# Leaving out 36 of the 70 clock-keeping products of an attention-and-expert kernel

## The chip, the cores and the metric

The kernel runs on one core of one Trainium2 chip. The metric is device time in microseconds of one execution. A core has a matmul engine (PE; its weight loads stand apart as PEld), VectorE (DVE), ScalarE (ACT), GpSimd (POOL) and SyncE (SP), each with its own instruction queue that is worked off in order, and DMA queues that move data. The engines wait for each other through semaphores. [...]

## The reference: what is computed

There are four batches of eight heads, each with 768 positions of 64 channels. For each head, six projected sign bits put every query and every key in one of 64 buckets, and a query attends only to the keys of its own bucket. The eight heads of a batch are laid side by side into rows of 512. Of each batch, the 128 rows with the highest gate score go through a two-layer expert and are added back.

In short:

```python
q_bits = (np.einsum('bhsd,dk->bhsk', q, proj) > 0).astype(np.int64)
k_bits = (np.einsum('bhsd,dk->bhsk', k, proj) > 0).astype(np.int64)
mask = q_bucket[:, :, :, None] == k_bucket[:, :, None, :]
scores = np.where(mask, scale * np.matmul(q, k.transpose(0, 1, 3, 2)), -1e9)
scores = scores - np.max(scores, axis=-1, keepdims=True)
attn = np.exp(scores); attn = attn / (attn.sum(-1, keepdims=True) + 1e-09)
x = np.matmul(attn, v)          # heads side by side: (4, 768, 512)
top_idx = np.argpartition(-(x[b] @ w_gate), 128)[:128]
out[b, top_idx] = xe + sigmoid(score) * (np.maximum(xe @ w1, 0) @ w2)
```

## The kernel before, in words

The 32 heads go through the same stages. In the **max pass** of a head (max_unit L649, max_relu L657, max_red L666) each of six row chunks takes two products of 128x384 into PSUM banks; ScalarE makes the tile me of one, and DVE joins it with the other and leaves the row maxima in one column of the tile M. The tiles me have two buffers, so the third me of a series waits until DVE has read the first. The maxima are turned into a row (row_first L462 for the first head, max_turn L676 for the others), which ScalarE copies into row 96 of the head's operand A (L466 for the first head). With that row in place come the **score products** (st_unit L697, L701), the exponentials on ScalarE (L715, L717), the low halves R on DVE and POOL (L732, L735) and the products with the values (av L760). The max pass of the next head is interleaved with the score and value products of this one. Four PSUM banks ("bank") serve the max pass, three ("st") the score products, one ("av") the values.

The first head has nothing to be interleaved with. While its inputs are still being split, PE computes its sign bits (hash_first L397) and those of the next heads (hash_half L476), and the max products come in between, as DVE and ScalarE let banks come free.

The **clock-keeping products** stand between these. `keep_warm` takes an st bank and calls `heat`, which multiplies a tile of ones by itself, 128x128 each time; nothing reads the result. There are six groups, of 34, 8, 8, 8, 6 and 6 products (in the trace: tile wq, L307). The group of 34 follows the first head's sign products. The three groups of 8 lie inside the first head's max pass. The two groups of 6 are PE's last instructions, behind the last product of the last batch's expert (down L993, tile yp).

The order of everything is written out by hand: a list of events is built once (`ev`), and the table `ORDER` names them by number in the order in which they are recorded. Each engine executes its share in that order. Leaving five events out of the list lowers the numbers behind them by five.

Of the kernel before, what the change touches and what calls it, by code (L numbers as in the profile page):

```python
# [44 lines left out]
WARM = (34, 8, 8, 8, 6, 6)  # L45
# [6 lines left out]
    0, 25, 8, 17, 31, 32, 33, 159, 9, 23, 15, 36, 10, 24, 26, 34, 91, 35, 309, 18, 158, 161, 308,  # L52
    28, 114, 163, 90, 1, 42, 92, 2, 44, 93, 164, 3, 160, 310, 95, 43, 94, 45, 96, 46, 48, 47, 99,
    -1, 97, 115, 102, 98, 49, 104, 100, 38, 107, 101, 103, 311, 106, 105, 12, 4, 165, 37, 166,
    110, 108, 20, 112, 22, 27, 111, 19, 29, 109, 39, 172, 113, 21, 16, 176, 173, 174, 178, 30,
    177, 314, 180, 120, 122, 192, 7, 179, 182, 124, 121, 123, 126, 116, 233, 128, 125, 175, 194,
    466, 130, 127, 117, 14, 181, 193, 162, 184, 129, 465, 118, 131, 5, 138, 11, 183, 264, 167,
    234, 136, 186, 140, 132, 119, 168, 133, 185, 188, 195, 187, 190, -1, 134, 189, 191, 13, 256,
    390, 260, 615, 261, 262, 143, 139, 258, 169, 170, 248, 252, 263, 144, 257, 146, 135, 145, 265,
    171, 147, 254, 259, 245, 137, 266, 148, 468, 244, 253, 141, 255, 150, 149, 196, 142, 246, -1,  # L60
    152, 198, 313, 315, -1, 197, 250, 316, 616, 241, 199, 200, 421, 247, 240, 202, 242, 151, 153,
    154, -1, 249, 201, 214, 471, 208, 267, 210, 155, 235, 209, 203, 236, 268, 243, 251, 211, 50,
    237, 334, 212, 238, 239, 326, 336, 204, 51, 213, 269, 217, 335, 327, 328, 337, 156, 338, 329,
    52, 330, 340, 339, 205, 323, 272, 206, -1, 270, 157, 218, 341, 207, 332, 53, 331, 220, 391,
    322, 271, 342, 765, 276, 273, 317, 219, 344, 221, 618, 278, 274, 215, 277, 312, 333, 915, 222,
    467, 216, 473, 343, 324, 397, 223, 280, 345, 325, 224, 275, 413, 470, 398, -1, -1, 225, 319,
    399, 318, 282, 320, 414, 321, 226, 227, 288, 279, 415, 229, 228, 401, 281, -1, 416, 230, 400,
    417, 290, 283, 403, 409, 232, -1, 346, 284, 231, 402, 472, 916, 404, 286, 419, 285, 347, 418,
    411, 289, 293, 410, 287, 420, 294, 405, 348, 295, 412, 422, 296, 407, 479, 392, 291, 499, 620,
    350, 480, 297, 299, 481, 500, 482, -1, 292, 298, 300, 301, 352, 349, 6, 351, 406, 501, 423,  # L70
    408, 358, 354, 364, 302, 303, 304, 393, 483, 394, 359, 502, 305, 353, 360, 541, 495, 355, 395,
    484, 485, 306, 486, 469, 424, 307, 356, 357, 487, 425, 361, 396, 540, 362, 491, 474, 493, 363,
    489, 368, 1223, 367, 365, 369, 371, 373, 488, 366, 427, 617, 496, 433, 490, 426, 370, 428,
    497, 492, -1, 429, 559, 548, 435, 498, 551, 430, 434, 494, 375, 552, 621, 553, 372, 431, 476,
    561, -1, 437, 619, 374, 475, 766, 436, 623, 432, 622, 438, 554, 377, 477, 376, 447, -1, 378,
    571, 379, 555, 547, 54, -1, 549, 445, 380, 441, 478, 550, 55, 382, 564, 381, 439, 556, 443,
    557, 1072, 450, 560, 446, 440, 558, 562, 503, 442, 768, 542, 451, 444, 563, 567, 453, 691,
    384, 565, 452, -1, 569, 56, 633, 504, 448, 383, 543, 507, 566, 57, 509, 638, 568, 505, 572,
    455, 457, 570, 637, 635, 510, 459, 385, 454, 449, 506, 515, 639, 770, 508, 544, -1, 545, 387,
    511, 456, 629, 634, 458, 461, 546, 521, 640, 460, 512, 631, 513, 630, 517, 641, 462, 649, 636,  # L80
    516, 514, 690, 632, 518, 643, 389, 645, 519, 646, 522, 579, 463, 577, 1073, 464, 520, 578,
    642, 525, 581, 523, 573, 651, 526, 524, 585, 528, 580, 650, 721, 624, 644, 647, 717, 582, 530,
    -1, 589, 648, 527, 697, 705, 652, 767, 532, 699, 719, 698, 595, 529, 590, 718, 700, 583, 626,
    625, 531, -1, 591, 771, 574, 627, 707, 584, 586, 706, 772, 713, 575, -1, 533, 769, 708, 592,
    534, 715, 536, 628, 720, 535, 701, 537, 587, -1, 593, 588, 597, 539, 714, 596, 576, 538, 594,
    653, 655, 702, 716, 654, 709, 600, 602, 773, 711, 601, 657, 722, 840, 656, 703, 603, 598, 599,
    604, 791, -1, 659, 658, 723, 671, 710, 605, 607, 783, 918, 712, 704, 660, 609, 606, 611, 785,
    608, 610, 692, 1222, 917, 661, 694, -1, 695, 784, 779, 612, 662, 663, 792, 781, 786, 793, 664,
    920, 665, 667, 780, 794, 693, 666, 613, 782, 696, 795, 668, 841, 669, 724, 388, 614, 739, 788,
    787, 797, 672, 921, 725, 727, 923, 670, 674, 386, 673, 675, 728, 677, 789, 676, 679, 678, 922,  # L90
    774, 1075, 796, 729, 726, -1, 798, 800, 855, 730, 680, 799, 790, 740, 681, 801, 731, 732, 857,
    733, 735, -1, 682, 683, 734, 1078, 847, 802, 856, 848, 849, 684, 736, 745, 919, 776, 777, 858,
    737, 775, 778, 741, 686, 685, 859, 738, 851, -1, 743, 850, 867, 687, 852, 871, 853, 868, 869,
    998, 864, 689, 803, 854, 747, 860, 870, 688, 804, 746, 863, 865, 750, -2, 751, 861, 866, 752,
    862, 945, 754, 753, 742, 805, 744, 806, 947, 809, 929, 842, 748, 811, 749, 843, 844, 807, 810,
    756, 931, 812, -1, 758, -2, 755, 757, 845, 808, 813, 846, 930, 58, 759, 761, 814, 59, 760,
    932, 762, 946, 872, 1074, 817, 933, 815, 60, 819, 1522, 935, 816, 950, 934, 818, 763, 924,
    885, 948, -1, 61, 873, 820, 949, 764, 821, 877, 937, 951, 822, 879, 825, -2, 823, 1028, 878,
    997, 952, 826, 827, 829, -2, 824, 828, 1225, 883, 941, 936, 880, 939, 942, 943, 884, 944, -2,
    830, 874, 881, 1080, 938, -1, 886, 925, 891, 940, 831, 1004, 1012, 926, 1077, 1076, 887, 833,  # L100
    927, 832, 882, 888, 1008, 835, 834, 928, 1079, 1014, 895, 889, 875, 890, 1006, 897, 836, 1013,
    955, 893, 1005, 896, 837, 1015, 892, -2, 959, 1017, 839, 1007, 876, 838, 1016, 1018, 900,
    1010, 901, 1009, 1024, 1086, 1019, 903, 1148, 1011, 960, 1025, 1026, 999, 894, 1088, 953, 902,
    -1, -2, 1020, -2, 1228, 954, 898, -2, 1029, 905, -2, 1373, 904, 1027, 907, 957, 961, 1147,
    1224, 956, 958, 1021, -2, -2, 971, 965, 909, 962, 906, 1022, 966, 963, 1000, 1090, -1, 899,
    1087, 964, 908, 910, 911, 1023, 1094, 1092, 1089, 1001, 1095, 967, 912, -2, -2, 1096, 1097,
    1098, 1002, -2, 913, 969, 1106, 1099, 914, 1091, 1100, 968, 975, 1003, -1, 1030, 1375, 1178,
    976, 1040, 970, 972, -1, 973, 1093, 978, 1034, 977, 1154, 979, 1101, 980, 1035, 1048, 1108,
    1107, 1229, 1102, 1041, 974, 1109, 1036, 1104, 1103, 1156, 1081, 982, 1105, 1155, 1158, 1037,
    1038, -1, 981, 1157, 1372, 1031, 1083, -2, 1227, 1082, 1162, 1039, 1164, 1046, 1042, 1167, -1,  # L110
    1160, 1230, 1084, 984, 1159, 1052, 986, 983, 985, 1032, 1047, 1161, 1166, 1049, 1043, 1168,
    987, 1053, 1169, 1044, 1050, 1045, 1054, 1175, 989, 1085, 1033, -2, 1110, 1124, 1523, 1297,
    -2, 988, 1174, 1236, 1163, 1176, 1057, 1177, 990, 1170, 1051, 1058, 1059, 1240, 1055, 1060,
    1112, 1378, 1061, 1111, 1298, 1056, 1172, 1171, 1122, 1165, 1179, 1113, 1123, 1063, 1062,
    1173, 1064, 1125, 1226, 1149, 1065, 1114, 1066, 1067, 1068, 1069, 1151, 1238, 1241, 1126,
    1374, 1115, 1242, 1243, 1116, 1152, 1150, 1237, 1128, 1117, 62, 1239, 64, 1118, 1308, -1,
    1071, 1070, 1248, 63, 1244, 1119, 1120, 1121, 65, 1132, 1133, 1135, 1153, 1246, -6, 1134,
    1245, 1127, 1129, 1186, 1231, 1310, 1130, 1180, 1247, 1196, 1136, 1380, 1131, 1184, 1197,
    1680, 1185, 1249, 1190, 1181, 1188, 1250, 1251, 1309, -6, -1, 1138, 1232, 1379, 1182, 1679,
    1137, 1139, 1187, 1257, 1256, 1140, 1258, 1142, 1311, 1141, -6, 1143, 1183, 1252, 1259, 1144,  # L120
    1192, 1316, 1253, 1191, 1198, 1189, 1324, 1254, 1317, 1193, 1318, 1194, -6, 1255, 1199, 1200,
    -1, 1319, 991, 1146, 1304, -6, 1326, 1305, 1299, -6, 1195, 1306, 1145, 1204, 1202, -1, 1233,
# [1186 lines left out]
```

## Time and profile before

| | |
|---|---|
| median of 3 runs | 411.87 us (411.31 to 412.36) |
| the profiled execution | 410.81 us, of which its span 408.6 us |
| PE busy | 389.4 us (95% of the span), 5738 products |
| DVE busy | 347.4 us (85%) |
| ACT busy | 332.2 us (81%) |
| POOL busy | 184.0 us (45%) |
| granted PE clock, mean | 1.00 |

The durations that follow are of the one profiled execution. The span runs from its first to its last instruction, and what the execution's own time has beyond it, 2.2 us, lies around it. A product that is followed by others shows a duration longer than the distance to the next start, because products overlap: for a run of them, the distance between starts is what each of them costs.

### The profile page before, as it was taken

How to read it: one execution, taken by the hardware profiler on the slowest of the kernel's cores; microseconds unless marked ns; L12 is line 12 of the kernel's file. 1: busy time of each engine (PE TensorE's matmuls, PEld its weight loads, DVE VectorE, ACT ScalarE, POOL GpSimd, SP SyncE). 2: the span in 40 equal slices, each digit the busy share in tenths (PEclk: the TensorE clock that was granted, in tenths of full speed). 3: DMA queues.
4: the chain of work that ended last, by engine and by line, in shares of the span. 5: the costliest groups of instructions: out<-in, count | busy, mean ns of one | idle time of the engine just before them, and what ended most of it. 6: DMA issues, size and time to landing. Idle time of an engine off the chain costs nothing.

```text
span 408.6 us, 14314 instructions
## 1 busy us (share of the span) xinstructions
PE 389.4 (95%) x5738; PEld 275.8 (68%) x5746; DVE 347.4 (85%) x928; ACT 332.2 (81%) x818; POOL 184.0 (45%) x105
## 2 busy tenths in 40 slices
PE   5799999999989999999999998999999999999995
PEld 3355776666756667687667765676677677778782
DVE  5998998998888998878889899999989988759942
ACT  5699999899989989897689987999899887757410
POOL 7737467466534466461523525335436260511010
PEclk9999999999999999999999999999999999999999
DMA  8475758655365666545455533834555354100030
GB/s 247 143 231 146 202 156 225 187 165 158 73 209 142 166 163 185 174 106 157 107 168 140 140 99 101 224 88 123 169 141 144 68 132 118 40 3 2 34 124 27
DMA packets 25586, 55.44 MB, mean 136 GB/s; under 512 B 3818, under 2 KB 10550, under 8 KB 25520
## 3 DMA queue, kind: packets, MB, share of 16 engines
q1 hardware_dynamic: 15104, 35.97, 33.9%
q10 hardware_dynamic: 9680, 16.45, 12.8%
q0 software_dynamic: 736, 2.11, 1.6%
q8 instruction: 45, 0.74, 0.7%
q14 instruction: 21, 0.17, 0.1%
HBM read 26.19 MB, written 7.35 MB: 82 GB/s over the span
## 4 chain that ended last, share of the span: by engine, by line
PE 75%; DVE 9%; issue 7%; ACT 5%; DMA 3%; POOLq 0%; SPq 0%; DVEq 0%; ACTq 0%
PE av L760 23%; PE st L697 14%; PE st L701 13%; PE bank L649 13%; PE bank L969 4%; PE bank L476 3%; PE bank L993 2%; DVE mj L666 2%; ACT me L657 1%; DVE R L732 1%; PE av L744 1%; ACT x L784 1%; DVE sel L896 1%; ACT P L715 1%; DVE cm L838 1%
## 5 line engine op out<-in xcount | busy, mean ns | idle before, releaser
L735 POOL TENSOR_TENSOR R<-P 128x1536 f16<-128x1536 f32 x46 | 134.1, 2918 | 158.9 <-DVE R L732 36.4
L760 PEld LDWEIGHTS <-P 128*128 128x128 bf16 x2304 | 127.2, 97 | 30.6 <-issue 4.3
L760 PE MATMUL av<-V,P 128*128 128x65 f16 (+2 forms) x2304 | 135.1, 194 | 0.1
L760 PE MATMUL av<-V,R 128*128 128x65 f16 (+1 forms) x1152 | 128.0, 193 | 1.0 <-DVE R L732 0.9
L666 DVE CUSTOM_DVE_ANT_0 mj<-bank,me 128x384 bf16<-128x384 f32 x192 | 102.4, 551 | 26.2 <-ACT me L657 12.0
L715 ACT ACTIVATE P<-st 128x512 f32<-128x512 f32 x192 | 113.2, 612 | 13.4 <-PE st L701 9.6
L697 PE MATMUL st<-A 97*128 97x512 f16 (+1 forms) x384 | 119.8, 326 | 1.7 <-DMA A<-mr 1.1
L701 PE MATMUL st<-B 128*128 128x512 f16 (+1 forms) x384 | 120.0, 326 | 0.0
L657 ACT ACTIVATE me<-bank 128x384 f32<-128x384 f32 x192 | 94.7, 505 | 24.0 <-PE bank L649 14.9
L649 PE MATMUL bank<-A 96*128 96x384 f16 x384 | 108.7, 326 | 2.2 <-DVE sg L493 0.9
L760 PEld LDWEIGHTS <-R 128*128 128x128 f16 x1152 | 107.3, 99 | 1.6 <-DVE R L732 1.5
L732 DVE TENSOR_TENSOR R<-P 128x768 f16<-128x768 f32 x100 | 100.1, 1016 | 3.2 <-ACT P L717 2.3
L717 ACT ACTIVATE P<-st 128x512 f32<-128x512 f32 x96 | 58.4, 615 | 2.1 <-PE st L701 1.7
L649 PEld LDWEIGHTS <-A 96*128 96x128 f16 x384 | 34.8, 98 | 24.6 <-issue 6.9
L697 PEld LDWEIGHTS <-A 97*128 97x128 f16 x384 | 37.4, 97 | 17.9 <-issue 3.8
L701 PEld LDWEIGHTS <-B 128*128 128x128 f16 x384 | 37.6, 98 | 15.9 <-issue 2.1
L784 ACT ACTIVATE x<-av,rc 128x64 f32<-128x64 f32 x192 | 44.0, 324 | 2.7 <-DVE rc L772 2.0
L513 DVE SCALAR_TENSOR_TENSOR T<-X,T 128x768 f16<-128x768 f32 x32 | 31.4, 988 | 0.0
L506 ACT ACTIVATE T<-X 128x768 f16<-128x768 f32 x32 | 27.6, 867 | 0.0
L821 POOL TENSOR_TENSOR w1l<-W,w1h 128x512 bf16<-128x512 f32 x8 | 13.8, 1730 | 10.9 <-PE st L701 5.8
L969 PEld LDWEIGHTS <-w1h 128*128 128x128 f16 x256 | 15.7, 97 | 1.3
L566 DVE SCALAR_TENSOR_TENSOR V<-V,V 128x768 f16<-128x768 f32 x16 | 16.4, 1022 | 0.0
(134 smaller groups left out, 412.4 us busy)
## 6 DMA issues: line engine op xcount, KB each, us to landing
X<-in_qk_dram SPq DMA_DIRECT2D x32, 384.0 KB
B<-T SPq DMA_DIRECT2D x62, 192.0 KB
A<-T SPq DMA_DIRECT2D x31, 240.0 KB
V<-in_v_dram ACTq DMA_DIRECT2D x16, 384.0 KB
out_dram<-x ACTq DMA_DIRECT2D x7, 768.0 KB
W<-in_w_dram ACTq DMA_DIRECT2D x8, 512.0 KB
sbc<-scores SPq DMA_DIRECT2D x3, 384.0 KB
out_dram<-x SPq DMA_DIRECT2D x1, 768.0 KB
```

Of the source, the lines that this page charges most:

```text
L649: nc.tensor.matmul(pt[:, :384], a[0][0:96, t * P : (t + 1) * P], a[1][0:96, 384:768] if i else K[h % NA][0:96], start=True, stop=True,)
L657: nc.scalar.activation(me, st["mx", h, t, 0][:, :384], AF.Relu)
L666: nc.vector.tensor_tensor_reduce(out=jk, in0=st["mx", h, t, 1][:, :384], in1=st["me", h, t], op0=ALU.add, op1=ALU.max, scale=1.0 / MS, sca ...
L697: nc.tensor.matmul(pt[:, o : o + n], a[1][:, c * P : (c + 1) * P], a[0][:, q0 : q0 + n], start=True, stop=False,)
L701: nc.tensor.matmul(pt[:, o : o + n], bt[:, 0, c * P : (c + 1) * P], bt[:, 1, q0 : q0 + n], start=False, stop=True,)
L715: nc.scalar.activation(pp[:, r, 0:512], pt, AF.Exp, scale=ES)
L717: nc.scalar.activation(pp[:, :, 512:768], pt.rearrange("p (a b) -> p a b", a=2), AF.Exp, scale=ES)
L732: mine(nc.vector.tensor_tensor(t[:, r], pp[:, r], hi_view(pp, r), op=ALU.subtract))
L735: turn(nc.gpsimd.tensor_tensor(t, pp, hi_view(pp, a), op=ALU.subtract))
L760: nc.tensor.matmul(o[:, t, o0:o1], l, vv[:, c, hh, v0 + o0 : v0 + o1], start=False, stop=last and l is lo, skip_group_check=True,)
L784: nc.scalar.activation(x[:, t], o[:, t, 1 : D + 1], AF.Copy, scale=rc[:, t : t + 1])
L969: nc.tensor.matmul(hp[:, f * P : (f + 1) * P], w[:, k, o : o + P], x[:, k * P : (k + 1) * P], start=(f == 0 and k == 0 and i == order[0]), ...
```

## The change

The list of groups is cut to the first one. The 24 products inside the first head's max pass and the 12 at the end go, each with its weight load: 36 products and 36 loads on PE, and nothing on any other engine. The table ORDER loses its five entries for them, and every number from 38 up is lowered by five.

```diff
-WARM = (34, 8, 8, 8, 6, 6)
+WARM = (34,)
...
 ORDER = (
...
-    -5, -8, -5, -8, -5, -5, -5, 41, 40,
...
+    -8, -5, -8, -5, -5, -5,
 )
```

PE's queue at the third group of 8, before. bank is a PSUM bank of the max pass, A_91 and A_92 are the operands of the first and the second head, wq is the clock-keeping products' bank:

```order
 L649 LDWEIGHTS A_91
 L649 MATMUL bank_66<-A_91 128x384 [waits Activation_49]
 L307 LDWEIGHTS ones_78
 L307 MATMUL wq_279<-ones_78 128x128 [waits PE_49]
...
 L649 LDWEIGHTS A_92 [waits DMAHW5_49,DMAHW2_49,DMAHW4_49,DMASW0_49,Pool_49]
 L649 MATMUL bank_65<-A_92 128x384 [waits Activation_49]
 L649 LDWEIGHTS A_92
 L649 MATMUL bank_67<-A_92 128x384 [waits Activation_49]
```

And the same place now:

```order
 L649 LDWEIGHTS A_91
 L649 MATMUL bank_66<-A_91 128x384 [waits Activation_49]
 L649 LDWEIGHTS A_92 [waits DMAHW5_49,DMAHW2_49,DMAHW4_49,DMASW0_49,Pool_49]
 L649 MATMUL bank_65<-A_92 128x384 [waits Activation_49]
 L649 LDWEIGHTS A_92
 L649 MATMUL bank_67<-A_92 128x384 [waits Activation_49]
```

The eight pairs are gone, and the second head's first max products follow the first head's last one directly, with the same banks and the same waits. At the first two groups it is alike.

PE's queue at its end before, where hth and htl are the expert's hidden layer in two parts and yp its result:

```order
 L993 LDWEIGHTS htl_8712
 L993 MATMUL yp_8771<-w2h,htl_8712 128x512
 L307 LDWEIGHTS ones_78
 L307 MATMUL wq_8799<-ones_78 128x128 [waits PE_49]
...
 L307 LDWEIGHTS ones_78
 L307 MATMUL wq_8806<-ones_78 128x128
 L1304 UNCONDITIONAL_BRANCH
```

And now:

```order
 L993 LDWEIGHTS htl_8685
 L993 MATMUL yp_8744<-w2h,htl_8685 128x512
 L1304 UNCONDITIONAL_BRANCH
```

The twelve pairs are gone, and PE's last instruction is the expert's last product.

## Rows read from the trace of the kernel before

**Rows 1.** The page's first part, busy time, share of the span and instructions of each engine, and of its second part the slices of PE and of the granted clock (tenths, 40 slices).

```profile
PE 389.4 (95%) x5738; PEld 275.8 (68%) x5746; DVE 347.4 (85%) x928; ACT 332.2 (81%) x818; POOL 184.0 (45%) x105
...
PE   5799999999989999999999998999999999999995
...
PEclk9999999999999999999999999999999999999999
```

**Rows 2.** The timeline of PE from its first product to the second group of 8: start, duration of the run, engine, line, operation, tiles, count, and in brackets PE's idle time before it with what ended it.

```profile
4.21 1.51 PE L397 MATMUL bank<-Xa,pjt 96*32 96x384 f32 x8 [4.21 <-DMA Xa<-in_qk_dram]
5.65 3.72 PE L307 MATMUL wq<-ones 128*128 128x128 f16 x34
9.56 0.48 PE L649 MATMUL bank<-A 96*128 96x384 f16 x2 [0.20 <-DVE A L418]
...
15.42 0.32 PE L649 MATMUL bank<-A 96*128 96x384 f16 x1 [0.91 <-DVE sg L493]
...
16.18 0.61 PE L307 MATMUL wq<-ones 128*128 128x128 f16 x8
```

**Rows 3.** The chain of waits from 16 us to the first score product, in order of time: start, duration, what the chain goes through.

```profile
16.00 0.57 DVE sg L493
16.59 0.37 DVE sg L499
16.98 0.36 DVE sg L500
17.37 0.56 DVE mj L666
17.94 0.47 DVE mj L666
18.42 0.25 DVE ident L350
...
18.71 0.33 PE bank L462 x3
19.04 0.17 PE bank L649
19.20 0.45 PE wq L307 x8
19.65 0.18 PE bank L649
19.86 0.43 ACT me L657
...
20.33 0.49 ACT me L657
20.85 0.48 ACT A L466
```

**Rows 4.** The timeline of all engines from 16.6 to 21.4 us, the same columns as Rows 2 (lines of POOL, SP and the weight loads are among those left out).

```profile
16.63 0.65 PE L649 MATMUL bank<-A 96*128 96x384 f16 x3
...
17.12 0.61 PE L307 MATMUL wq<-ones 128*128 128x128 f16 x8
...
18.00 0.32 PE L649 MATMUL bank<-A 96*128 96x384 f16 x1 [0.26 <-DVE M L666]
18.04 0.97 ACT L657 ACTIVATE me<-bank 128x384 f32<-128x384 f32 x2 [0.43 <-DVE M L666]
...
19.04 0.61 PE L307 MATMUL wq<-ones 128*128 128x128 f16 x8
19.08 0.47 ACT L466 CAST A<-bank 1x384 f16<-1x384 f32 x1
19.19 0.56 DVE L666 CUSTOM_DVE_ANT_0 mj<-bank,me 128x384 bf16<-128x384 f32 x1 [0.53 <-PE bank L462]
19.49 0.65 PE L649 MATMUL bank<-A 96*128 96x384 f16 x3
...
19.67 0.55 DVE L666 CUSTOM_DVE_ANT_0 mj<-bank,me 128x384 bf16<-128x384 f32 x1
19.86 0.97 ACT L657 ACTIVATE me<-bank 128x384 f32<-128x384 f32 x2 [0.30 <-PE bank L649]
...
21.37 0.38 PE L697 MATMUL st<-A 97*128 97x512 f16 x1 [0.17 <-ACT A L466]
```

**Rows 5.** The end of the timeline.

```profile
402.46 1.03 PE L993 MATMUL yp<-w2h,htl 128*128 128x512 f16 x4
...
403.32 0.83 PE L307 MATMUL wq<-ones 128*128 128x128 f16 x12
403.52 0.75 DVE L1000 SCALAR_TENSOR_TENSOR ye<-yp,ss,xe 128x512 f32<-128x512 f32 x1 [2.63 <-PE yp L993]
404.55 0.98 POOL L1001 DMA_INDIRECT out_dram<-ye,idx  x1 [8.42 <-DVE ye L1000]
```

**Rows 6.** PE by stretches: the stretch, its length, PE's busy time with the count of products, granted clock, share and rate of the DMA engines. The stretch from 14.2 to 21.4 us stands in the table of all products here.

```profile
4.20:9.40 5.20, 5.16 (x42) 1.00 1.01 333
...
14.20:21.40 7.20, 4.96 (x46) 1.00 0.62 186
```

**Rows 7.** The same stretch of 7.2 us, the clock-keeping products (L307) alone.

```profile
14.20:21.40 7.20, 1.83 (x24) 1.00 0.62 186
```

**Rows 8.** PE by stretches at the end, the same columns.

```profile
404.20:406.00 1.80, 0.00 (x0) 1.00 0.00 0
...
408.20:408.40 0.20, 0.00 (x0) 1.00 0.00 0
408.40:408.60 0.20, 0.00 (x0) 0.74 0.00 0
```

**Rows 9.** The first 8 us of score products and value products, busy time of each engine with the count (PE, PEld, DVE, ACT, POOL), granted clock, DMA share and rate.

```profile
21.40:29.40 8.00, 7.81 (x71) 4.57 (x70) 7.60 (x21) 7.71 (x18) 3.47 (x2) 1.00 0.77 219
```

**Rows 10.** The timeline of PE at its longest wait behind the first head, the same columns as Rows 2.

```profile
251.69 0.22 PE L676 MATMUL bank<-ident,M 128*128 128x128 f16 x1 [1.43 <-DVE W L622]
...
252.33 0.27 PE L697 MATMUL st<-A 97*128 97x256 f16 x1
252.44 0.27 PE L701 MATMUL st<-B 128*128 128x256 f16 x1
```

318 rows, old and new, of the table ORDER are left out of this document.

## The prediction

> **What bounds the kernel now.** I read the page's busy times first, then the chain of waits, then the timeline of the two places where the removed products stand, and last the stretches with PE's busy time and its granted clock. The busy times show PE at 95% of the span [rows 1]: over most of the kernel what PE executes sets the time, and a product less would be time gained. The slices say where that is not so: the first slices stand at 5, 7 and 9 tenths, the last at 5, and 24 of the removed products lie in the second and third slice, 12 in the last. Both places are those in which PE waits for others.
>
> In the first place the chain shows who is waited for [rows 3]. From 16.00 to 18.67 us it is DVE alone, one instruction behind the other. Then come three transposing products, a max product, the third group of clock-keeping products (0.45 us), a max product, two me copies on ACT, and the copy that writes the row into A; at 21.37 us the first score product starts, and it had waited for that copy [rows 4]. From there PE is the bound: 7.81 of the next 8.00 us are busy [rows 9]. So a change in the first head's max pass is worth what it does to 21.37 us. At the other end DVE starts the last result at 403.52 us, when the last real product has ended (402.46 + 1.03 = 403.49), while the 12 products still execute until 404.15 us [rows 5].
>
> **The change part by part.** A run of 8 products takes 0.61 us with the last one's drain, which also stands in each run: with 0.22 us for a single product of this shape [rows 10], (0.61 - 0.22) / 7 = 0.056 us from start to start. A group therefore holds PE for 8 x 0.056 = 0.45 us, which is also what the chain shows for the third; the three hold it for 1.34 us of the 1.83 us that they show as busy [rows 7]. The 12 hold it for 0.83 - 0.22 = 0.61 us and one more distance, 0.67 us. These are the most that can be gained, 2.0 us, if all of it were waited for.
>
> First group, 16.18 to 16.63 us [rows 2, 4]. The three max products behind it start 0.45 us earlier at best. Their readers are DVE and ACT. DVE is in the unbroken row of the chain from 16.00 us [rows 3], so it comes to these banks no earlier. ACT's next me copies start at 18.04 us after a wait for DVE, for there are two me buffers [rows 4]. Cost on the path 0, gain 0.
>
> Second group, 17.12 to 17.6 us. The max product behind it starts at 18.00 us and had itself waited 0.26 us for DVE [rows 4]. Without the group it waits 0.71 us. Gain 0.
>
> Third group, 19.04 to 19.49 us. This is the one that stands in the chain [rows 3]. The second head's first max product starts at 19.49 us behind it, and ACT's me copy at 19.86 us is put down to that product, after 0.30 us of idling [rows 4]. Without the group the product could end before ACT is free of the row copy at 19.55 us (19.08 + 0.47), and the 0.30 us looks like a gain. But that me is the third of its series: it needs the buffer that DVE reads from 19.19 to 19.75 us. The two other such releases show what comes between DVE's end and ACT's start: 19.67 + 0.55 = 20.22 us to the second copy at 20.33 us, 0.11 us, and 19.75 + 0.11 is 19.86 us, the very start that the row has. So both releasers come together within hundredths, and with the product gone early DVE is the one that is late. DVE in turn starts at 19.19 us after the transposing products, which stand ahead of the group in PE's queue. Gain 0, at most the 0.30 us if the buffer is not what I take it for.
>
> The 12 at the end. DVE waits for the tile yp, not for wq, and what follows is DVE, POOL's scatter issue at 404.55 us and its transfer to 408.6 us [rows 5]. PE's queue ends 4.4 us ahead of the span's end with the group, and about 5 us without. Gain 0.
>
> The sum is 0.0 us. The profiled execution took 410.81 us (span 408.6 us and 2.2 us around it) and lies 1.06 us below the median of the runs; the change is set against the median 411.87 us, so the forecast is 411.9 us.
>
> What hides the cost of the removal is the clock. The products do no work, but they are a part of PE's activity: in the 7.2 us from 14.2 to 21.4 us PE is busy 4.96 us with them [rows 6], and 4.96 - 1.83 = 3.13 us, 43%, without [rows 7]. [...]
>
> The trace does not show so thin a stretch, so its cost is bounded from both sides. Nothing: PE stood entirely idle from 404.15 us, the rows say 1.00 until 408.4 us, and only then 0.74, a fall within the last 0.2 us [rows 8], so 4.3 us of idling went ahead of it. Without the groups the longest idle stretch is the 0.91 us that is already there, and a wait of 1.43 us in the middle left the distances of the score products behind it at 0.11 us for 256 columns [rows 10]. The other end is the fall in this stretch, priced below at 0.15 to 2.7 us. I take nothing, as the rows on idling are nearest.
>
> [...]
>
> **The rivals.** Slower: the clock falls in the first head. The place is PE between 14.2 and 21.4 us, and it decides when the level is low as the score products begin. For it speaks that the removed products were over a third of PE's busy time there (1.83 of 4.96 us); against it, 4.3 us of level kept in full idleness. Price: before 21.37 us only the three transposing products are on the path, 3 x (0.106 - 0.056) = 0.15 us. From 21.37 us PE is the bound, and if the level comes back as at the start, after 5.16 us of work, half of these are lost, 2.6 us. ACT and DVE are busy 7.71 and 7.60 of the 8 us there [rows 9], so neither makes it good. Sum 0.15 us if the level is back by then, 2.7 us if not: 412.0 to 414.6 us, mostly the latter.
>
> Faster: PE's queue was the bound after all. The chain names the third group, 0.45 us [rows 3]; a me buffer or a bank that comes free earlier than I read would give its 0.3 to 0.45 us, 411.4 to 411.6 us. If what waits on DVE were itself late because of the first two groups, up to 1.34 us, and with the end's 0.67 us up to 2.0 us, 409.9 us. Against it: the waits for DVE in [rows 4], and the DVE row without a break in [rows 3].
>
> The groups don't do what they are called: that is the forecast itself for the 24, which then keep nothing, and it is sure for the 12, behind which no product stands.
>
> **How the numbers follow.** Nothing on the path and no fall: 0.58, 411.9 us. A fall: 0.28, of which 0.03 stay below 0.3% (1.2 us, about what a measurement of this kernel can tell from no change). A gain on PE's queue: 0.14, of which 0.10 above 0.3%, since a shifted order in the first head can carry into later waits. So same is 0.58 + 0.03 + 0.04 = 0.65, slower 0.25, faster 0.10. The forecast alone has 411.3 to 412.4 us, the spread of the runs before. The range takes in the fall up to 414.5 us, and below it half of the gain, down to 410.8 us; about 0.06 and 0.08 are left out.
>
> **What would show it.** If the steps hold, the first score product starts at 21.4 us within 0.2 us, the second head's first me copy is put down to DVE instead of PE, PE's idle time in the first head grows by about 1.3 us, and the score products behind it keep their distance of 0.22 us for 512 columns. The DVE instruction of the last result starts 0.03 us behind the last yp product, and PE's level falls some 0.6 us earlier at the end. A granted clock below 1.00, or score products 0.43 us apart from 21 us on, would show the fall; a start before 21.1 us the gain. Wrong would be a time above 413.1 us or below 410.6 us.

## The result, and the profile after

| | before | after |
|---|---|---|
| median of 14 runs each, on one chip | 411.75 us (410.46 to 412.68) | 414.21 us (412.31 to 417.04) |
| ratio, 95% interval | | 1.0064 (1.0041 to 1.0087) |
| the profiled execution | 410.81 us, span 408.6 us | 413.71 us, span 411.5 us |
| mean granted clock of the profiled execution | 1.00 | 0.991 |

The change makes the kernel slower by 0.64%. The forecast was 411.9 us. The time lies inside the range (410.8 to 414.5 us) only because the range takes in a rival; it lies above 413.1 us, which the prediction itself named as a sign of being wrong. The likeliest case, no change, did not come; the rival that was given 0.28 did: PE's clock falls in the first head. Of all runs below, three (two of the kernel before, one of e5) took over 1.5% longer than the fastest of their kernel; the ratios, and the counts of runs by their clock, leave them out.

The page after, the same lines as [rows 1]; in the second and third slice the clock has lost a digit or two:

```profile
PE 390.4 (95%) x5710; PEld 273.8 (67%) x5710; DVE 347.1 (84%) x928; ACT 332.9 (81%) x818; POOL 184.3 (45%) x105
...
PE   4699999999989999999999998999999999999995
...
PEclk9879999999999999999999999999999999999999
```

PE executes 36 products fewer (the loads fall by 36; of the products of before, eight have no record), and its busy time is 1.0 us longer. The stretches after (columns as in [rows 6]: length, PE's busy time with the count, granted clock, DMA) place the low level:

```profile
17.00:18.00 1.00, 0.58 (x3) 0.99 0.09 19
18.00:19.00 1.00, 0.48 (x1) 0.50 0.47 125
...
24.00:25.00 1.00, 1.00 (x7) 0.60 0.20 53
25.00:26.00 1.00, 1.00 (x8) 1.00 0.27 61
```

The profile gives the granted clock as a share of full speed: it is 1.00 until 18.0 us, 0.50 until 24.8 us (the low level in what follows), and 1.00 again. PE's timeline over the same time, to be set against [rows 2, 4]:

```profile
4.52 1.51 PE L397 MATMUL bank<-Xa,pjt 96*32 96x384 f32 x8 [4.52 <-DMA Xa<-in_qk_dram]
5.96 2.90 PE L307 MATMUL wq<-ones 128*128 128x128 f16 x34
9.88 0.48 PE L649 MATMUL bank<-A 96*128 96x384 f16 x2 [1.01 <-DVE A L418]
...
15.74 0.32 PE L649 MATMUL bank<-A 96*128 96x384 f16 x1 [0.91 <-DVE sg L493]
16.34 0.32 PE L649 MATMUL bank<-A 96*128 96x384 f16 x1 [0.28 <-DVE M L666]
16.93 0.65 PE L649 MATMUL bank<-A 96*128 96x384 f16 x3 [0.27 <-DVE sg L493]
18.32 0.48 PE L649 MATMUL bank<-A 96*128 96x384 f16 x1 [0.73 <-DVE M L666]
19.04 0.48 PE L462 MATMUL bank<-ident,M 128*128 128x128 f16 x3 [0.24 <-DVE ident L350]
19.31 1.57 PE L649 MATMUL bank<-A 96*128 96x384 f16 x4
...
21.84 0.59 PE L697 MATMUL st<-A 97*128 97x512 f16 x1
22.23 0.63 PE L701 MATMUL st<-B 128*128 128x512 f16 x1
22.65 0.63 PE L697 MATMUL st<-A 97*128 97x512 f16 x1
```

A single max product takes 0.32 us until 17 us and 0.48 us from 18 us on. The score products that stood 0.22 us apart (21.37 and 21.59 us before) stand 0.39 to 0.43 us apart. Between the first product and the fall no idle stretch is longer than 1.01 us; that one ends at 9.88 us, 8 us ahead of the fall. In the 4 us ahead of the fall the longest is 0.91 us, and that one is there before the change too.

Where the 2.9 us between the two profiled spans lie is read by taking one instruction of each head, the product that opens its bank of value products (L744), in both timelines. The first head's, before and then after:

```profile
27.38 0.33 PE L744 MATMUL av<-W,zs 128*128 128x396 f16 x1
...
29.27 0.33 PE L744 MATMUL av<-W,zs 128*128 128x396 f16 x1
```

0.31 us are there already at the first product, which waits for the inputs (4.52 against 4.21 us); at the first head's L744 the difference is 1.89 us; at the second 2.13 us; it stays within 0.1 us of that for ten heads; 0.5 us come at 148 to 159 us and 0.4 us between 307 and 327 us, and the last head has 2.95 us. So 1.8 us of the 2.9 arise between 4.5 and 42 us, the stretch with the low level. In the profiles of e2 and e10, which also lack the three groups, it is 1.75 us each by the second head. The later steps come with the clock at 1.00. Such steps are there without any fall too: of the 1.3 us by which e1's profiled span exceeds the one before, 1.1 us come between 72 and 84 us. The last step of the changed kernel is this wait:

```profile
319.52 0.39 PE L697 MATMUL st<-A 97*128 97x512 f16 x1 [0.65 <-DMA A<-mr]
```

### The profile page after: what moved, and what is told of

The parts are those of the page before. It is cut to its first block, busy times and chain, and to the rows that moved or that the text cites. A ratio compares the mean times of both kernels' runs of the same rounds, so it can differ in the third digit from the quotient of the medians.

```text
span 411.5 us, 14249 instructions
## 1 busy us (share of the span) xinstructions
PE 390.4 (95%) x5710; PEld 273.8 (67%) x5710; DVE 347.1 (84%) x928; ACT 332.9 (81%) x818; POOL 184.3 (45%) x105
## 4 chain that ended last, share of the span: by engine, by line
PE 70%; DVE 9%; ACT 8%; issue 7%; DMA 4%; POOLq 0%; SPq 0%; DVEq 0%; ACTq 0%
PE av L760 21%; PE st L697 13%; PE st L701 12%; PE bank L649 12%; PE bank L969 4%; PE bank L476 3%; PE bank L993 3%; DMA A<-mr 2%; DVE mj L666 2%; ACT me L657 2%; ACT x L784 2%; ACT P L715 2%; DVE R L732 1%; PE av L744 1%; ACT P L717 1%
## 5 line engine op out<-in xcount | busy, mean ns | idle before, releaser
L657 ACT ACTIVATE me<-bank 128x384 f32<-128x384 f32 x192 | 94.8, 506 | 24.8 <-PE bank L649 14.0
L649 PE MATMUL bank<-A 96*128 96x384 f16 x384 | 109.9, 330 | 3.6 <-DVE sg L493 1.2
```

The source lines that it names most:

```text
L649: nc.tensor.matmul(pt[:, :384], a[0][0:96, t * P : (t + 1) * P], a[1][0:96, 384:768] if i else K[h % NA][0:96], start=True, stop=True,)
L657: nc.scalar.activation(me, st["mx", h, t, 0][:, :384], AF.Relu)
```

## The experiments

All kernels but e10 are the kernel before with the counts of the groups changed, and e9 and e11 have one more group elsewhere; a group of 0 is left out. In the table `WARM` the second entry stands at the second place in the first head, the third entry at the first place. None of these products enters the output.

**Which of the 36 products.** e1_end_out, with `WARM = (34, 8, 8, 8, 0, 0)`:

> Only the 12 products at the end are left out; the three groups of 8 stay. Theory (all of the 2.5 us come from PE's clock, which falls in the first head without the groups): the same as before, 411.3 to 412.3 us, mean granted clock 1.00. Rival (the 12 at the end matter, for the next execution or for the end of the program): 413 us or more, or a clock below 1.00 at the start.

Measured: 411.68 us (410.71 to 413.20) against 411.79 us of the kernel before in the same job, ratio 0.9994 (0.9970 to 1.0018). The profiled run stays at 1.00 until 409.8 us, 0.1 us ahead of its end; 4 of the 12 runs have a mean granted clock of 0.996 or less, against 13 of 34 of the kernel before in this job. No worth of the 12 at the end is seen; the interval leaves room for 0.3% in loss and 0.2% in gain.

e2_groups_out:

```diff
-WARM = (34, 8, 8, 8, 6, 6)
+WARM = (34, 0, 0, 0, 6, 6)
```

> Only the three groups of 8 are left out; the 12 at the end stay. Theory (clock): the same as the changed kernel, 413 to 415.5 us, with a stretch of about 7 us at a granted clock of 0.50 in the first 30 us. Rival (the 12 at the end): 411.8 us and a clock of 1.00.

Measured: 413.19 us (412.62 to 415.61), ratio 1.0033 (1.0006 to 1.0059). All 12 runs have a mean granted clock between 0.987 and 0.992; of the kernel before in this job, no run of 34 is below 0.993. Its profile:

```profile
17.50:18.00 0.50, 0.00 (x0) 0.83 0.49 126
18.00:24.50 6.50, 6.23 (x23) 0.50 0.74 224
24.50:25.00 0.50, 0.50 (x4) 0.84 0.20 63
```

The low level lasts as long as in the changed kernel, 6.8 us. So the loss belongs to the 24 products in the first head.

e10_changed_again, the changed kernel itself:

> The changed kernel once more, beside the others on one chip, because leaving out the three groups alone gave 413.2 us and the changed kernel 414.2 us in another job. If the 12 products at the end are worth nothing: 413.2 us within 0.6 us, all runs with a fall in the first head. If they are worth 1 us when the groups are gone: 414 us or more.

Measured: 412.69 us (412.10 to 414.90), ratio 1.0024 (1.0009 to 1.0039), all 12 runs between 0.988 and 0.994. That is 0.5 us below e2, which ran in another job on another chip, so the 12 at the end do not show a worth of 1 us when the groups are gone either. It is also 1.5 us below the first measurement of the same kernel, and the clocks say why in part. There the mean clocks of the 14 runs go from 0.996 down to 0.980. With a low level of 0.50, as the stretches show it, the low time is by estimate 2 x (1 - clock) x span: 2 x 0.020 x 414.8 = 16.6 us in the run of 417.04 us, 2 x 0.005 x 410.1 = 4.1 us in that of 412.31 us. Runs with the same clock still differ by 3.6 us (413.35 and 416.92 us at 0.988), so the clock isn't all of it. How long the low level lasts, or how often it comes, differs from run to run and from job to job, and the price of the change with it: 0.24 to 0.64%.

**How many, and where.** e3_third_out, with `WARM = (34, 8, 8, 0, 0, 0)`:

> The third group of 8 and the 12 at the end are left out; the first two groups stay. My step on the third group (0.45 us of PE in the chain, but the me copy behind it waits for DVE at the same time): if the clock stays, the first score product starts as before within 0.1 us behind the transposing products, and the time is 411.5 to 412.2 us. Rival (the third group is on the path): 0.3 us earlier, 411.4 us. If the third group is needed for the clock as well: 413 to 415 us with a stretch at 0.50.

Measured: 411.51 us (410.57 to 414.75), ratio 1.0000 (0.9973 to 1.0026). Its profile, timeline and stretches:

```profile
16.07 0.32 PE L649 MATMUL bank<-A 96*128 96x384 f16 x1 [0.28 <-DVE M L666]
16.23 0.61 PE L307 MATMUL wq<-ones 128*128 128x128 f16 x8
...
19.66 0.53 PE L649 MATMUL bank<-A 96*128 96x384 f16 x2 [0.23 <-ACT A L466]
...
21.42 0.39 PE L697 MATMUL st<-A 97*128 97x512 f16 x1 [0.17 <-ACT A L466]
21.64 0.60 PE L701 MATMUL st<-B 128*128 128x512 f16 x1
```

```profile
18.00:21.50 3.50, 2.42 (x14) 1.00 0.76 197
21.50:22.00 0.50, 0.50 (x2) 0.65 0.84 307
22.00:25.00 3.00, 3.00 (x11) 0.50 0.71 222
25.00:25.50 0.50, 0.50 (x4) 0.94 1.02 221
```

Two answers. Up to the first score product the clock is high, the product at 16.07 us is 0.05 us later than before (16.02), and the score product at 21.42 us also 0.05 us (21.37): leaving out the third group gains 0.00 us, as the step said, although the chain of before ran through it. And in this run the level falls after all, at 21.65 us, 3.7 us later than in the changed kernel's profile and behind the piece that the group had filled. In the median of the runs that does not show, and whether the missing group caused this fall is open.

e4_one_of_24, with `WARM = (34, 0, 24, 0, 0, 0)`:

> The 24 products stand in one group of 24 at the place of the first (16.2 us), none at the other two places; the 12 at the end are left out. If the amount of PE work between 14 and 21 us decides: a clock of 1.00 and 411.8 to 412.6 us (the group takes 24 x 0.056 = 1.34 us, up to 0.9 us of it late for the products behind it, most of it under DVE's work). If the spread decides, because the stretch from 17.5 us on is thin again: a fall, 413 to 415 us.

Measured: 411.73 us (410.73 to 413.76), ratio 1.0006 (0.9980 to 1.0031), and the profile has no fall in the first head. The time fits the first expectation: 24 products in one place do as well as in three. The mean clocks of the 12 runs, 0.992 to 0.999, cannot confirm it, since without the 12 at the end they hold a fall behind the last product too (here from 408.6 us to the end, 411.3 us). The profile showed something else, a fall in the middle of the kernel:

```profile
250.00:254.50 4.50, 2.97 (x48) 1.00 0.04 9
254.50:255.00 0.50, 0.50 (x7) 0.97 0.00 0
255.00:258.00 3.00, 3.00 (x20) 0.50 0.24 55
258.00:258.50 0.50, 0.50 (x4) 0.61 0.99 214
```

Here is the wait of 1.43 us [rows 10] in this run:

```profile
253.28 0.22 PE L676 MATMUL bank<-ident,M 128*128 128x128 f16 x1 [1.43 <-DVE W L622]
```

The level falls at 254.97 us, 1.7 us after the end of the wait, and it costs: the difference to the kernel before at L744 is 1.60 us at 241 us and 2.74 us at 267 us, 1.14 us for 3.4 us at the low level.

e5_half, with `WARM = (34, 4, 4, 4, 0, 0)`:

> Three groups of 4 in place of 8, at the same places, the 12 at the end left out. If the fall goes by how much PE works in the first head: some runs fall there and some not, mean granted clocks between 0.990 and 1.000, a median of 411.8 to 413 us. If any product that breaks up the waits is enough: as with 8, 411.3 to 411.9 us, no stretch at 0.50 before 30 us. If 4 are as good as none: all runs at 0.992 or less, 413 us or more.

Measured: 412.46 us (411.01 to 420.56), without the longest run 412.30 us, ratio 1.0000 (0.9974 to 1.0026): the time does not tell it from before. Four of the other 11 runs are at 0.992 or less (one or two of 12 in e1, e3, e4 and e6), and the profile has the fall in the first head:

```profile
16.00:19.00 3.00, 1.87 (x14) 1.00 0.36 110
19.00:19.50 0.50, 0.20 (x1) 0.74 0.24 46
19.50:26.00 6.50, 6.41 (x27) 0.50 0.77 223
26.00:26.50 0.50, 0.50 (x4) 0.93 0.00 0
```

By the mean clocks some runs fall and some do not, as the first of the three expectations has it; the mean does not say where a fall lies. The waits that the products break up are the same as with 8, so breaking up the waits was not enough in this run.

e6_double, with `WARM = (34, 16, 16, 16, 0, 0)`:

> Three groups of 16 in place of 8 (0.9 us of PE each), the 12 at the end left out. This prices the products themselves. If PE's queue has room for them in the first head (the waits for DVE are 0.3 to 0.9 us): the first score product is late by at most 0.5 us, 411.5 to 412.3 us, no fall in the first head. Rival (every product in the chain counts): 24 x 0.056 = 1.3 us, 413.1 us.

Measured: 412.60 us (411.30 to 415.57), ratio 1.0025 (1.0005 to 1.0044), with no fall in the first head of the profile. The time is above the first expectation and below the rival's. Here the products do reach the path:

```profile
16.27 0.32 PE L649 MATMUL bank<-A 96*128 96x384 f16 x1 [0.28 <-DVE M L666]
...
19.29 1.06 PE L307 MATMUL wq<-ones 128*128 128x128 f16 x16
20.19 0.65 PE L649 MATMUL bank<-A 96*128 96x384 f16 x3
...
21.97 0.38 PE L697 MATMUL st<-A 97*128 97x512 f16 x1 [0.17 <-ACT A L466]
```

From the product at 16.27 us to the first score product are 5.70 us; before it is 21.37 - 16.02 = 5.35 us. The second 8 of each group cost 0.35 us together, the first 8 nothing. The other 0.4 us of the median are not explained by this profile.

**Is it the same at 250 us?** e9_guard is e1 with 20 products put ahead of the transposing product of head 21 (event 1690 of the order), which waits for DVE there:

```diff
-WARM = (34, 8, 8, 8, 6, 6)
+WARM = (34, 8, 8, 8, 0, 0)
...
-    1766, 1594, 1690, 1646, 1769, 1768, 1689, 1691, -3, 1771, 1777, 1661, 1657, 1659, 1655, -3,
+    1766, 1594, 2519, 1690, 1646, 1769, 1768, 1689, 1691, -3, 1771, 1777, 1661, 1657, 1659, 1655, -3,
...
-    gens = [
+    at(keep_warm, 9, 20); gens = [
```

> The three groups of 8 stay, the 12 at the end are left out, and 20 products (1.1 us of PE) are put ahead of the transposing product of head 21, where PE waits 1.4 us for DVE at 250 us. Theory: the fall at 255 us, seen in one profile, is the same mechanism and is in about half of the runs of the kernel before (17 of 35 have a mean granted clock of 0.997 or less); with the products it is gone: at most 2 of 12 runs at 0.997 or less, median 411.0 to 411.4 us. Rival (the falls in the runs of before lie elsewhere): the same share of such runs, 411.8 us. Rival (the products delay what they stand ahead of): no such runs, but 412 us or more.

Measured: 411.41 us (410.58 to 413.02), ratio 0.9993 (0.9977 to 1.0008). Three of 12 runs are at 0.997, one more than expected, none lower; the profiled run is one of the three, and its only fall is behind the last product (406.2 us to the end). Its timeline at the place:

```profile
250.34 1.28 PE L307 MATMUL wq<-ones 128*128 128x128 f16 x20
251.93 0.22 PE L676 MATMUL bank<-ident,M 128*128 128x128 f16 x1 [0.32 <-DVE W L622]
```

The wait has shrunk from 1.43 to 0.32 us, the products fit into it, and nothing behind them is later (L744 differs from before by 0.24 us on both sides). The limit of 0.997 was badly drawn, because a fall at the end reaches it, as this profile shows. Of runs at 0.996 or less there are none of 12 here and 9 of 34 of the kernel before in the same job.

e11_before_guard, the same 20 products with `WARM` as before, so that the 12 at the end keep that count clean:

> The kernel before with all its clock-keeping products, and the 20 products ahead of the transposing product of head 21 besides. With the 12 at the end kept, a mean granted clock of 0.996 or less can only be a fall in the middle. Theory: none or one of 12 runs at 0.996 or less (24 of 70 runs of the kernel before), median 411.2 to 411.6 us, and no run between 412.5 and 414 us. Rival (the earlier dozen was luck, or the 20 products delay): four or more runs at 0.996 or less, or a median of 411.9 us or more.

Measured: 411.27 us (410.48 to 414.34) against 411.88 us, ratio 0.9982 (0.9953 to 1.0012). Two of 12 runs are at 0.996 or less, between the two expectations; of the kernel before in the same job it is 3 of 17. The profiled run is one of the two, and its fall lies elsewhere again, ahead of the max pass:

```profile
8.00:11.00 3.00, 1.44 (x20) 1.00 0.89 294
11.00:11.50 0.50, 0.40 (x2) 0.70 0.29 111
11.50:14.50 3.00, 3.00 (x10) 0.50 0.28 75
```

In both kernels together 2 of 24 runs have such a clock, against 12 of 51 of the kernel before in the same two jobs: too few to tell. Over the three jobs, the runs of the kernel before with 0.996 or less have a median of 412.46 us (25 of 85 runs), the other 60 one of 411.47 us. The medians with the 20 products are 0.4 and 0.6 us below before, but neither ratio is clear of 1: the version may be better, and is not shown to be. Nor is it shown that the falls in the runs of before lie at 255 us: e4's profile is the only one of eleven that has one there.

## Why the prediction was right or wrong

**The 36 products hold no other engine up: right.** The three groups and the 12 at the end were costed at 0 on the path. For the third group e3 shows it to the hundredth. For the first two e10 does, while its clock is still at 1.00: from the max product ahead of the first group to the one behind the second are 1.97 us (16.04 to 18.01 us), before 1.98 us. For the 12, e1 shows nothing against it. The reason given for the third, that the me copy would then wait for DVE, stands in the profile after, and so at 19.91 us in e3, where the clock is still at 1.00:

```profile
20.33 0.97 ACT L657 ACTIVATE me<-bank 128x384 f32<-128x384 f32 x2 [0.30 <-DVE M L666]
```

The 0.30 us is the wait of [rows 4], with DVE named in place of PE. e6 shows the edge of it: the room is used up somewhere between 8 and 16 products a group. One reading was off without weight in the sum: a slice is 10.2 us, so all 24 products (16.18 to 19.65 us) lie in the second slice, none in the third. At the end DVE starts 0.03 us behind the last yp product, as said:

```profile
405.35 1.03 PE L993 MATMUL yp<-w2h,htl 128*128 128x512 f16 x4
406.41 0.75 DVE L1000 SCALAR_TENSOR_TENSOR ye<-yp,ss,xe 128x512 f32<-128x512 f32 x1 [2.63 <-PE yp L993]
```

**The clock stays: wrong.** This is the step that failed: "I take nothing, as the rows on idling are nearest." Two readings led to it. The first took the 4.3 us of full idleness at the end [rows 8] as a sign of how much idling it takes. In eight of the eleven profiles the level falls behind the last product, 2.2 us (e5) to 5.0 us (e1) after that product's end, so one profile gave one draw of a time that varies; that it is less by 2 us in another run could not be seen in the one trace at hand. The second took the wait of 1.43 us without a fall [rows 10] as a proof that such a place is safe. e4 has the same wait and a fall 1.7 us after it, and by the mean clocks 25 of 85 runs of the kernel before fall somewhere. The nearest row to a stretch with many short waits was none of those on long idling. In the first head 24 products were 1.83 of 4.96 us of PE's busy time [rows 6, 7]. Without them the level fell there in all three profiled runs of the two kernels that lack them, with no idle stretch above 1.01 us behind the first product. Of their 38 runs every one has a mean clock of 0.996 or less, and 32 have 0.992 or less; of the 85 runs of before it is 25 and 1. In the first profile after, PE idled 0.91, 0.28 and 0.27 us in the 4 us ahead of the fall, the fall came within an idle stretch of 0.73 us, and the low time was 6.8 us.

The profiles alone would not show that the 24 products decide, because they also differ in something else. The 34 products at the start take 2.87 to 3.29 us in the six runs whose level falls before 22 us (the changed kernel twice, e2, e3, e5, e11), and 3.54 to 3.81 us in the five others. The kernel before has them 0.106 us apart, (3.72 - 0.22) / 33 [rows 2]; the changed kernel has the first 18 of them 0.102 us apart (5.96 to 7.80 us) and the other 16 0.056 us, (1.06 - 0.22) / 15. The granted clock stands at 1.00 over all of them in both profiles; that the level had risen earlier in the six is an estimate from these distances. e11 has every group and falls too, at 11.2 us. How far the moment of that first rise decides where a later fall comes is not shown; it is another reason not to read much from one profile of e3, e4 or e5. What shows the worth of the 24 products is the 38 runs and the medians.

**The price of the fall: right in its bounds, with one part mis-sized.** 0.15 us was set for what comes late up to the first score product. Its 0.106 us for a product at the low level is the distance of the first 34 [rows 2], where the granted clock stands at 1.00, so that the level was low there is an estimate from the distance. In e5 the third group's four products take 0.43 us (20.18 to 20.61 us), 0.107 us each, at a granted clock of 0.50. The first score product starts 0.47 us later than before, of which 0.31 us are the later inputs: 0.16 us. 2.6 us was set for half of 5.16 us of low level from there on, PE's busy time at the start of the kernel [rows 6]. No run shows a level that comes back after 5.16 us of work. It came back 3.0 us after the first score product's start (21.84 to 24.8 us), and half of that, by the score products at 0.43 in place of 0.22 us, is 1.5 us. The sum measured at the first head's L744 is 1.89 - 0.31 = 1.58 us, against 1.6 us from these two parts. So the low level lasted longer than assumed, 6.8 us against 5.16 us, but 3.8 us of it lay ahead of the first score product, where only 0.16 us was paid. The medians of the three measurements lie 0.9 to 2.5 us above before, on both sides of the 1.8 us that the profiles show by the second head; what moves them is not explained. The other part of the profiled 2.9 us is later waits: the one for the transfer A<-mr at 319.5 us is found in all five profiles with a fall between 17 and 22 us and in none of the six others, but why is open.

**"PE's idle time grows by about 1.3 us": wrong with the clock.** PE is busy 4.87 of the 7.30 us from 14.5 to 21.8 us, nearly as before (4.96 of 7.20 us), since at the granted clock of 0.50 the real products (0.48 in place of 0.32 us for a single max product) fill the time of the removed ones.

**The other rivals.** No gain on PE's queue was seen in any kernel. That the groups keep nothing is refuted for the 24; for the 12 nothing speaks against it. The sign given for the end, a fall of the level some 0.6 us earlier, came with 0.9 us (410.5 us, 1.0 us ahead of the span's end, against 0.1 us), but with falls 2.2 to 5.0 us behind the last product it tells nothing.

## What to carry to other kernels

A clock-keeping product is not costed by its own time alone but by what the clock does without it: here the time rose by 0.24 to 0.64% without products whose removal gained 0.01 us at most on the path. Ask in which stretch PE is busy for less than the rest of the kernel (here 3.13 of 7.2 us without the 24, against 95% of the span), even if no single wait there is long (0.91 us at most), and what is PE-bound directly behind it (7.81 of the next 8.00 us). A single profile in which the clock stayed high is one draw; the mean granted clock of every run shows how often it falls (0.996 or less in 25 of 85 runs of the kernel before), and the falls hide in the spread of a kernel's times. Before such products are removed as useless, or placed elsewhere, leave them out group by group. In this kernel's waits they cost nothing until they filled them: the second 8 of each group cost 0.35 us together, the first 8 nothing.

## What the runs showed of the hardware that was not expected

The low level came 8 us after the last wait above 0.91 us (the changed kernel), and a level that had held through 1.43 us of idling in the run before fell 1.7 us after the same wait in e4. With PE fully idle behind its last product, the level fell after 2.2 us in one run (e5) and after 5.0 us in another (e1). The low levels ahead of that lasted 3.4 us (e3, e4, e11) or 6.8 us (the changed kernel, e2, e5, e10), although PE was busy for 6.24 of the 6.8 us in the changed kernel. The kernel before has falls of its own: 25 of 85 runs at a mean clock of 0.996 or less, 1.0 us slower in the median than the others.
